# Reordering the second quad's scores and the sums in the first two attention stages of a fused attention and MLP kernel

## The chip, the cores and the metric

The kernel runs on one core of a Trainium2 chip. The metric is the device time of one execution in microseconds (us); lower is better. Engines: PE is TensorE (matrix products), ACT is ScalarE, DVE is VectorE, POOL is GpSimd, SP is SyncE, which here only issues the stores of the result.

## The reference

Attention with 32 global and 512 local tokens for 8 batches of 8 heads, and behind it a two-layer MLP with a sigmoid gelu. The attention output of a batch (544 rows of 8 x 64) is the MLP's input. Local tokens see the global keys and the local keys within 32 positions; global tokens see everything.

```python
k_all = concat([k_g, k_l], axis=2); v_all = concat([v_g, v_l], axis=2)
out_g = softmax(scale * q_g @ k_all.T) @ v_all
s_ll = where(abs(pos[:, None] - pos[None, :]) <= 32, scale * q_l @ k_l.T, -1e9)
s_l = concat([scale * q_l @ k_g.T, s_ll], axis=-1)
out_l = softmax(s_l) @ v_all
x = concat([out_g, out_l], axis=2).transpose(0, 2, 1, 3).reshape(B * S, H * D)
h = x @ w_in                                # 512 -> 2048
g = h * (1 / (1 + exp(-1.702 * h)))
out = g @ w_out                             # 2048 -> 512
```

## The kernel before

The four heads of half a batch are a "quad". A quad stands for its heads on the four groups of 32 partitions. In the code `a` is the first quad of the batch in work and `c` the second. The kernel's own order of calls is the order of each engine's queue: nothing is rescheduled, and an engine that waits holds up everything behind it in its queue. Waits are placed by the tile framework, from which tiles an instruction reads and writes.

The steps of a quad:

- `T`, `Tq`, `Tk`, `ext` (DVE, some copies on ACT): queries and keys as loaded (`rq`, `rk`) are transposed and laid out; the global ones come from `qgT` and `kgT`.
- `S(rnd)` (PE): scores of the local keys in two rounds, into four PSUM banks, one for each head. In batch 0 (class `Quad`) `B(rnd)` puts a bias there first, with products by an identity, and `S` adds to it (`added=True`). A score target is either a pair of two-bank tiles (`spair()`, tags s0 and s1; `bank(pair, j)` is bank j % 2 of tile j // 2), or, with `split=True`, four single banks.
- `X(rnd)` (ACT): exponentials out of PSUM into the tile `e`, which is `E[rnd]`: two instructions on a pair, four on single banks.
- `M(rnd, eng)` (DVE unless told otherwise): from batch 1 on (class `Wide`) the exponentials are multiplied by a mask of ones and zeros.
- `U(unit)` (PE): unit 0 multiplies the exponentials by ones, which gives the softmax sums; units 1 and 2 multiply them by the two halves of the values. Batch 0 has global keys apart: `K` (scores), `XK` (exponentials), `ekU(unit)` (their share of each unit, accumulated in the same bank).
- `R` (DVE): transpose `sT` out of the bank of unit 0, reciprocal `rT`, transpose `rs`.
- `XL(h)` (DVE): bank of unit 1 + h times `rs`, into the MLP's input `xL`.
- `eg`, `Gm`, `G`: the same for the 32 global queries.

PSUM has eight banks: four singles that rotate (`pbank`, tag p), and the pairs s0 and s1, one buffer each. A new tile in a buffer waits until the old one has been read.

The MLP of a batch follows as sixteen hidden tiles (`h_mm` into a bank, L611; `gelu` into `gT`, L616), each the sum of four products of 512 columns, and the second product (`o_mm`, L651; from batch 2 on a scheme with fewer products, L722). While the second product of batch i runs, the attention steps of batch i + 1 are called between its parts (`osteps`); `o_out` copies a finished tile of the output out of PSUM, and SP issues its stores.

Loads are issued by POOL. `behind(c.E[1][...])` (L624) is a one-element copy on POOL that reads the second quad's masked exponentials, so that the loads called after it (batches 2 and 3) are issued only when these are done. Their `rk` and `rq` go through `Tk`, `Tq` and `transpose_g`; the first quad's `ext` of batch 2 is on ACT between the gelus of batch 1.

Lines that the text names: L335 `B`, L352 and L556 `S`, L371 `K`, L380, L383 and L567 `X`, L407 `XK`, L419 `ekU`, L434 and L582 `U`, L452 and L593 `Gm`, L458 to L462 `R`, L467 `XL`, L572 `M`, L508 `Tk`, L772 the copy of an output tile on DVE, L81 and L82 the loads of `rq` and `rk`, L225 the copies that build the mask, L113 a copy on ACT.

Of the kernel before, what the change touches and what calls it, by code (L numbers as in the profile page):

```python
# [20 lines left out]
def kernel(  # L21
# [12 lines left out]
    nc = tc.nc  # L34
# [246 lines left out]
    def spair():  # L281
        return [psS.tile([128, 2, 512], F32, name="s4", tag="s%d" % i) for i in range(2)]

    def bank(pair, j):
        return pair[j // 2][:, j % 2, :]
# [358 lines left out]
    def o_mm(i, st, out=True):  # L644
        tci, f4 = divmod(st, 4)
        first = (i, tci) not in ops
        if first:
            ops[i, tci] = pbank("op")
        op = ops[i, tci]
        for fc in range(4 * f4, 4 * f4 + 4):  # L650
            nc.tensor.matmul(op, lhsT=gTs[i][:, fc, tci * 128 : tci * 128 + 128],  # L651
                             rhs=w_out_sb[:, fc, :], start=(first and fc == 4 * f4), stop=(fc == FC - 1))
        if f4 == 3 and out:
            o_out(i, tci, op)
# [102 lines left out]
    def tile_out(i, tci, ob, engs=4 * (nc.sync,), cols=slice(0, d_model)):  # L757
        for j, eng in enumerate(engs):
            if i < B:
                rows = out[i * S + Sg : (i + 1) * S, cols].rearrange("(r t) m -> t r m", t=16)[4 * tci + j]  # L760
            else:
                r = (4 * tci + j) * S
                rows = out[r : r + Sg, cols]
            eng.dma_start(out=rows, in_=ob[32 * j : 32 * j + 32])
# [3 lines left out]
    def o_out(i, tci, op, copy=on_act):  # L768
        if tci % 2 == 0:
            obs[i, tci // 2] = moe.tile([128, 4, HM], F32, name="ob", bufs=3)  # L770
        ob = obs[i, tci // 2][:, tci % 2 * 2 : tci % 2 * 2 + 2].rearrange("p h m -> p (h m)")
        copy(ob, op)  # L772
        tile_out(i, tci, ob)

    a, c = Quad(0), Quad(1)
# [35 lines left out]
    c.B(0)  # L811
    a.K()
    a.XK()
    c.S(0, added=True)
    c.X(0)
    a.eg()
    a.U(0)
    a.ekU(0)
    a.R()
    pt = spair()  # L820
    c.B(1, split=True, more=[bank(pt, 0)])
    c.S(1, split=True, added=True)
    c.X(1)
    a.ekU(1)
    a.U(1)
    a.XL(0)
    c.K()
# [6 lines left out]
    pt = spair()  # L834
# [22 lines left out]
    def osteps(i, *sts):  # L857
        for tci, f4 in sts:
            o_mm(i, 4 * tci + f4)

    nq = {1: (Wide(2), Wide(3)), 2: (Wide(4), Wide(5))}
    a, c = nq[1]
# [19 lines left out]
    c.S(0)  # L882
    c.X(0)
    osteps(0, (0, 3), (1, 3))
    c.M(0)
    o_mm(0, 11, False)
    o_out(0, 2, ops[0, 2], nc.vector.tensor_copy)
    c.S(1)
    c.X(1)
    for unit in range(3):  # L890
        a.U(unit)
    a.R()
    c.M(1)
    behind(c.E[1][0:1, 0, 32:34])
    load(2, (0,))
# [3 lines left out]
    load_v(2)  # L899
    osteps(0, (3, 2), (3, 3))  # L900
    pt = spair()
    a.XL(0)
    a.XL(1)
    a.Gm(bank(pt, 1)[:, 0:128])
    c.Gm(bank(pt, 1)[:, 128:256])
    c.U(0, bank(pt, 0))
    c.R()
    c.U(1, bank(pt, 2))
    c.U(2, bank(pt, 3))
    c.XL(0)  # L910
    c.XL(1)
    gTs[1] = moe.tile([128, FC, TB], BF16, name="gT")
# [9 lines left out]
    pt = spair()  # L922
# [3 lines left out]
    a, c = nq[2]  # L926
# [154 lines left out]
    for i in range(1, B):  # L1081
        if i > 1:
            for fc in range(FC):
# [3 lines left out]
                if i + 1 < B:  # L1087
                    c = nq[i + 1][1]
# [108 lines left out]
```

## Time and profile before

| | |
|---|---|
| median of 3 runs | 291.94 us (291.76 to 292.04) |
| profiled execution, its own time | 292.44 us |
| span of the profiled execution, first to last instruction | 290.4 us |
| PE busy | 277.3 us, 95% |
| DVE busy | 204.2 us, 70% |
| ACT busy | 184.2 us, 63% |
| POOL busy | 94.0 us, 32% |
| mean granted PE clock | 0.995 |

Times in the profile count from the first instruction of the span. The attention of batch 0 takes the first 18 us, its hidden layer lasts to about 33 us, its second product with the attention of batch 1 to about 52 us, and the hidden layer of batch 1 to about 67 us. A timeline row gives start, duration, engine, line, operation, output<-inputs, shapes and how many instructions were merged; the idle time of the engine before it is in brackets, with what ended it. Some records of matrix products are missing, so that a row can show one product too few.

### The profile page before, as it was taken

The page shows a single profiled execution, that of the slowest core. Times are in us where ns is not written, and L with a number is a line of the kernel's source. Part 1 is how long each engine was busy: PE and PEld are TensorE (multiplying, and loading weights), DVE is VectorE, ACT ScalarE, POOL GpSimd, SP SyncE. Part 2 cuts the span into 40 slices and gives each one's busy share as a digit, 9 for nine tenths or more (in the row PEclk, how much of TensorE's full clock was granted, in tenths as well). Part 3 has the DMA queues.
Part 4 walks back from the last instruction along what each step waited for, and adds up shares of the span by engine and source line. Part 5 has one row for each costly group of instructions (what it writes and reads, how often), then busy time and mean ns, then how long its engine had stood idle before and what let it go on. Part 6 is the DMA issues. An engine that isn't in the chain of part 4 may idle for free.

```text
span 290.4 us, 8836 instructions
## 1 busy us (share of the span) xinstructions
PE 277.3 (95%) x3704; PEld 178.5 (61%) x3727; DVE 204.2 (70%) x494; ACT 184.2 (63%) x296; POOL 94.0 (32%) x140
## 2 busy tenths in 40 slices
PE   6899999999999999999999999999999999999990
PEld 5544445544554488647874588548864787468880
DVE  7670456788689898679957995889865885454360
ACT  4747747388778684878658765878477834763330
POOL 8884550766946003910095006600210000000000
PEclk9999999999999999999999999999999999999998
DMA  7999993999999802991169503910121012200232
GB/s 200 160 205 211 203 140 58 156 224 134 157 187 157 146 3 68 94 194 30 34 75 175 106 5 75 144 21 2 48 72 30 2 29 67 54 2 0 75 85 61
DMA packets 59736, 28.23 MB, mean 97 GB/s; under 512 B 47665, under 2 KB 50225, under 8 KB 59697
## 3 DMA queue, kind: packets, MB, share of 16 engines
q0 software_dynamic: 51664, 17.57, 55.1%
q1 hardware_dynamic: 7552, 9.45, 11.9%
q8 instruction: 29, 0.48, 0.7%
q10 hardware_dynamic: 480, 0.66, 0.7%
q14 instruction: 11, 0.08, 0.1%
HBM read 36.31 MB, written 8.91 MB: 156 GB/s over the span
## 4 chain that ended last, share of the span: by engine, by line
PE 90%; DVE 2%; DMA 2%; POOL 1%; issue 1%; ACT 1%; DVEq 0%; POOLq 0%
PE hp L611 37%; PE px L722 13%; PE py L722 9%; PE op L651 9%; PE x L722 6%; PE s L556 6%; PE ov L582 5%; PE s L611 2%; DMA rk<-in_k_l_dram 2%; DVE xL L467 1%; ACT e L380 1%; PE og L593 1%; DVE rs L462 0%; DVE sT L458 0%; PE s L352 0%
## 5 line engine op out<-in xcount | busy, mean ns | idle before, releaser
L611 PE MATMUL hp<-xL,w_in_sb 128*128 128x512 bf16 x465 | 104.7, 379 | 1.2 <-DVE xL L467 0.4
L611 PEld LDWEIGHTS <-w_in_sb 128*128 128x128 bf16 x576 | 56.1, 98 | 60.4 <-issue 0.7
L616 ACT ACTIVATE gT<-hp 128x512 bf16<-128x512 f32 x120 | 69.8, 597 | 20.8 <-PE hp L611 19.3
L567 ACT ACTIVATE e<-s 128x1016 bf16<-128x1016 f32 (+1 forms) x56 | 53.3, 1003 | 22.9 <-PE s L556 22.9
L722 PEld LDWEIGHTS <-gs 128*128 128x128 bf16 x480 | 46.2, 98 | 6.5
L695 DVE TENSOR_TENSOR gs<-gT 128x512 bf16<-128x512 bf16 (+1 forms) x90 | 30.3, 364 | 17.4 <-ACT gT L616 17.2
L572 POOL TENSOR_TENSOR e<-e,mask 128x1760 bf16<-128x1760 bf16 x4 | 13.3, 3318 | 82.6 <-ACT e L567 82.6
L98 POOL DMA_DIRECT2D v<-in_v_l_dram x40 | 31.2, 784 | 15.9 <-DMA rk<-in_k_l_dram 5.3
L722 PE MATMUL py<-wsum,gs 128*128 128x256 bf16 x240 | 30.3, 273 | 0.0
L572 DVE TENSOR_TENSOR e<-e,mask 128x1712 bf16<-128x1712 bf16 (+1 forms) x24 | 25.0, 1043 | 6.9 <-ACT e L567 6.9
L651 PE MATMUL op<-w_out_sb,gT 128*128 128x512 bf16 x122 | 28.8, 380 | 0.5 <-issue 0.3
L508 DVE STREAM_TRANSPOSE kT<-rk 128x512 f32<-128x512 f32 x14 | 14.6, 1046 | 14.7 <-DMA rk<-in_k_l_dram 14.7
L651 PEld LDWEIGHTS <-gT 128*128 128x128 bf16 x128 | 11.8, 98 | 13.9
L722 PEld LDWEIGHTS <-gT 128*128 128x128 bf16 x192 | 18.0, 98 | 2.7
L722 PE MATMUL px<-w_out_sb,gT 128*128 128x256 bf16 x160 | 19.2, 273 | 0.0
L722 PE MATMUL px<-w_out_sb,gs 128*128 128x256 bf16 x160 | 19.1, 273 | 0.0
L467 DVE TENSOR_TENSOR xL<-ov,rs 128x512 bf16<-128x512 f32 x27 | 17.9, 686 | 0.8 <-PE ov L434 0.4
L692 DVE TENSOR_TENSOR gs<-gT 128x1024 bf16<-128x1024 bf16 (+1 forms) x30 | 17.4, 578 | 0.0
L556 PEld LDWEIGHTS <-kT 32*128 32x128 bf16 x672 | 12.6, 93 | 7.3 <-issue 5.9
L113 ACT ACTIVATE ob<-px 128x512 f32<-128x512 f32 x10 | 6.0, 597 | 15.2 <-DVE zz L744 15.2
L556 PE MATMUL s<-q,kT 32*128 32x160 bf16 (+1 forms) x448 | 15.0, 246 | 0.0
L100 POOL DMA_DIRECT2D v<-in_v_g_dram x24 | 14.0, 584 | 1.7 <-DMA rq<-in_q_l_dram 1.7
(149 smaller groups left out, 341.2 us busy)
## 6 DMA issues: line engine op xcount, KB each, us to landing
out_dram<-ob SPq DMA_DIRECT2D x128, 64.0 KB, 2.6
rq<-in_q_l_dram POOLq DMA_DIRECT2D x5, 512.0 KB, 8.3
rk<-in_k_l_dram POOLq DMA_DIRECT2D x5, 512.0 KB, 10.3
v<-in_v_l_dram POOLq DMA_DIRECT2D x24, 96.0 KB, 4.6
w_in_sb<-in_moe_w_in_dram POOLq DMA_DIRECT2D x8, 256.0 KB, 7.4
w_out_sb<-in_moe_w_out_dram POOLq DMA_DIRECT2D x4, 512.0 KB, 10.0
rq<-in_q_l_dram POOLq DMA_DIRECT2D x5, 256.0 KB, 8.4
rk<-in_k_l_dram POOLq DMA_DIRECT2D x5, 256.0 KB, 7.9
```

Source lines behind the costliest of these rows:

```text
L98: nc.gpsimd.dma_start(out=vt[0:n, hs, c, :D], in_=vs[FIRST[c] : FIRST[c] + n, hs])
L467: nc.vector.tensor_mul(self.x[:, 2 * self.u + h, :], self.st[1 + h], self.st["rs"])
L508: nc.vector.transpose(flat[:, 0:Sl].rearrange("p (r t) -> p t r", t=16), loaded[self.b][0][:, self.u].bitcast(F32))
L556: nc.tensor.matmul(bank(self.ps, j)[:, at : at + n], lhsT=self.k[p, KEYS[c] : KEYS[c] + 128, e], rhs=qs[p, :, :, e], start=(e == 0), stop= ...
L567: nc.scalar.activation(self.E[rnd][:, 2 * i : 2 * i + 2, :n], self.ps[i][:, :, :n], AF.Exp, scale=scale)
L572: eng.tensor_mul(e, e, mask[:, rnd : rnd + 1, :n].to_broadcast([128, 4, n]))
L611: nc.tensor.matmul(hp[:, : width(i)], lhsT=w_in_c[:, fc // 4, kc, fc % 4 // 2, :, fc % 2], rhs=(xL[i] if i < B else xG)[:, kc, :], start=( ...
L616: nc.scalar.activation(out_, in_, AF.Gelu_apprx_sigmoid)
L651: nc.tensor.matmul(op, lhsT=gTs[i][:, fc, tci * 128 : tci * 128 + 128], rhs=w_out_sb[:, fc, :], start=(first and fc == 4 * f4), stop=(fc = ...
L692: nc.vector.tensor_tensor(sums[i][2][:, g, :n], t[:, g, 0, :n], t[:, g, 1, :n], ALU.add)
L695: nc.vector.tensor_tensor(sums[i][k][:, g, : n // 2], x[:, g], y[:, g], op)
L722: nc.tensor.matmul(out_, lhsT=lv[:, g, tt * 128 : tt * 128 + 128], rhs=rv[:, g, :], start=(g == 0 and k in ((1, 3, 4, 6) if self.apart els ...
```

## The change

In batch 0 most bias products of `c`'s second score round are called ahead of `c.S(0)`, the rest and the second round itself directly after it. The first quad's sums follow behind that round. The first quad's three accumulators lie in a score pair; the four single banks go to the second quad's scores. `ekU(unit)` comes ahead of `U(unit)` in unit 0 as well.

In the second product of batch 0, where the attention of batch 1 is computed, `c.M(0)` runs on POOL. `a.U(0)` and `a.R()` are called ahead of `c.S(1)`, and `a.XL(0)` ahead of `c.M(1)`. The two `Gm` are called after the second quad's units.

```diff
@@ batch 0
     c.B(0)
     a.K()
     a.XK()
+    c.B(1, split=True, js=range(3))
     c.S(0, added=True)
     c.X(0)
-    a.eg()
-    a.U(0)
-    a.ekU(0)
-    a.R()
-    pt = spair()
-    c.B(1, split=True, more=[bank(pt, 0)])
+    c.B(1, split=True, js=(3,))
     c.S(1, split=True, added=True)
     c.X(1)
-    a.ekU(1)
+    a.eg()
+    pt = spair()
+    a.ekU(0, bank(pt, 0))
+    a.U(0)
+    a.R()
+    a.ekU(1, bank(pt, 1))
     a.U(1)
     a.XL(0)
     c.K()
     c.XK()
     a.ekU(2, bank(pt, 2))
     a.U(2)
     a.XL(1)
     a.Gm()
@@ batch 0's second product
     c.S(0)
     c.X(0)
     osteps(0, (0, 3), (1, 3))
-    c.M(0)
+    c.M(0, nc.gpsimd)
     o_mm(0, 11, False)
     o_out(0, 2, ops[0, 2], nc.vector.tensor_copy)
+    a.U(0)
+    a.R()
     c.S(1)
     c.X(1)
-    for unit in range(3):
-        a.U(unit)
-    a.R()
+    a.U(1)
+    a.U(2)
+    a.XL(0)
     c.M(1)
     behind(c.E[1][0:1, 0, 32:34])
     load(2, (0,))
...
     load_v(2)
     osteps(0, (3, 2), (3, 3))
     pt = spair()
-    a.XL(0)
     a.XL(1)
-    a.Gm(bank(pt, 1)[:, 0:128])
-    c.Gm(bank(pt, 1)[:, 128:256])
     c.U(0, bank(pt, 0))
     c.R()
     c.U(1, bank(pt, 2))
     c.U(2, bank(pt, 3))
+    a.Gm(bank(pt, 1)[:, 0:128])
+    c.Gm(bank(pt, 1)[:, 128:256])
     c.XL(0)
     c.XL(1)
```

## The prediction

> **What bounds the kernel now.** I read the page first: TensorE (PE) is busy 95% of the span, and section 4 gives it the chain.
>
> ```profile
> span 290.4 us, 8836 instructions
> ...
> ## 4 chain that ended last, share of the span: by engine, by line
> PE 90%; DVE 2%; DMA 2%; POOL 1%; issue 1%; ACT 1%; DVEq 0%; POOLq 0%
> ```
>
> So only what stops PE, or starts a long run of its products later, can move the end. Next, who PE waits for (columns: total us, times, longest); after the first kernel stage one wait is left, on VectorE (DVE):
>
> ```profile
> engine line waited for: us in total, times, longest us
> PE s L352 <- DVE q L313: 1.9, 1, 1.9
> ...
> PE s L352 <- DVE eg L393: 0.6, 1, 0.6
> PE hp L611 <- DVE xL L467: 0.4, 1, 0.4
> ```
>
> The 0.6 lies where the first edit is, the 0.4 where the second is. Third, the timeline of the first place (start, length, engine, line; in brackets the idle time before):
>
> ```profile
> 9.86 1.82 ACT L380 ACTIVATE e<-s 128x428 bf16<-128x428 f32 x4
> 11.76 0.66 PE L352 MATMUL s<-q,kT 32*128 32x200 bf16 x16 [0.55 <-DVE eg L393]
> 12.46 1.66 ACT L383 ACTIVATE e<-s 128x856 bf16<-128x856 f32 x2 [0.29 <-PE s L352]
> 13.11 0.81 PE L335 MATMUL s<-bias,ident 128*128 128x192 bf16 x8
> 13.22 0.72 DVE L458 STREAM_TRANSPOSE sT<-ov 128x512 f32<-128x512 f32 x1 [1.47 <-PE ov L419]
> 14.46 0.40 PE L419 MATMUL ov<-ek,rvg 32*32 32x512 bf16 x4
> 14.54 1.81 ACT L380 ACTIVATE e<-s 128x428 bf16<-128x428 f32 x4 [0.42 <-PE s L352]
> 16.89 0.40 PE L419 MATMUL ov<-ek,ones 32*32 32x512 bf16 x4 [0.16 <-ACT ek L407]
> ```
>
> ScalarE (ACT) idles 0.42 ahead of the second quad's second exponentials, waiting for its scores: that is what the first edit addresses. Fourth, the second place and what hangs on it:
>
> ```profile
> 47.67 0.68 DVE L772 COPY ob<-op 128x512 f32<-128x512 f32 x1
> 50.12 1.01 DVE L572 TENSOR_TENSOR e<-e,mask 128x1712 bf16<-128x1712 bf16 x1
> 51.20 0.17 POOL L624 COPY spot_p<-e 1x2 bf16<-1x2 bf16 x1 [8.04 <-DVE e L572]
> 51.97 0.55 POOL L82 DMA_DIRECT2D rk<-in_k_l_dram  x1
> 54.84 1.89 PE L611 MATMUL hp<-xL,w_in_sb 128*128 128x512 bf16 x8 [0.45 <-DVE xL L467]
> 59.06 1.06 DVE L508 STREAM_TRANSPOSE kT<-rk 128x512 f32<-128x512 f32 x1 [2.35 <-DMA rk<-in_k_l_dram]
> 61.52 0.31 ACT L113 ACTIVATE q<-qgT 128x128 bf16<-128x128 bf16 x1 [1.08 <-DVE qgT L243]
> 62.85 0.59 ACT L616 ACTIVATE gT<-hp 128x512 bf16<-128x512 f32 x1
> 63.49 0.38 PE L611 MATMUL hp<-xL,w_in_sb 128*128 128x512 bf16 x1
> ```
>
> Read it upwards. The last row is the first product of hidden tile 12 of batch 1; it takes the PSUM bank of tile 8, whose gelu (62.85) ends at 63.44. PE issues a product each 0.216 (16 of them take 3.62, less 0.38 for the last) and would have been there at 63.47, so this place is level, without slack. That gelu stands in ACT's queue behind L113, which waited for qgT, behind kT on DVE, which waited for the DMA of rk. That DMA was issued behind POOL's one-element copy L624, which waits for the second quad's second mask product (50.12 to 51.13). So **when c.M(1) ends** sets PE at 63.49, whatever PE gains at 54.84.
>
> **First edit, the scores of c in batch 0.** No instruction is added. Six of the eight bias products of c.B(1) now go ahead of c.S(0), two behind it; a's sums, their reciprocal R and c's second round change places, and a's three accumulators move from single banks into the score pairs.
>
> Start of c.S(0): the four single banks rotate; c.B(1)'s third product needs the bank that a.X(1)'s fourth exponential reads, to 9.86+1.82=11.68. With 0.05 from an end to PE's start (the bias product at 10.02 follows an exponential that ended at 9.97) it runs at 11.73; three more of 0.07 to 0.08 and 0.16 for the change to the score shape put c.S(0) at 12.11, not 11.76: +0.35. The 0.55 idle before it covers only the first two.
>
> X(0) moves to 12.81-14.47. X(1) no longer waits for its scores and follows at 14.36: -0.18. a.ekU(0) waits for the first half of X(0) (13.69) and runs at 13.74; a.U(0) follows 0.32 later and ends at 14.56. R's first transpose takes 14.61-15.33.
>
> Now the step that decides. a.ekU(1) writes bank 1 of the pair whose bank 0 that transpose reads, and stands after it in the program. The framework orders accesses by tile, and the pair is one tile: the product gets a wait for the transpose. In the kernel before these sums lie in tiles of their own. No row of before shows such a wait, so its bounds are 0 (ordered by bank, start at 14.50) and 0.88 (start at 15.38, from 15.33+0.05); I take the upper, since that is how tiles are declared here. Queued behind it on PE are a.U(1), c.K, a.ekU(2), a.U(2), a.Gm, c.U(0) and c.ekU(0). In the trace PE alone needs 16.66-14.46=2.20 from a.ekU(1) to c.ekU(0) (16.50, the last c.U(0) product, and 0.16). So c.ekU(0) comes at 17.58, against 16.89. ACT's exponential of c.K would end at 17.44: hidden. The first layer of batch 0 then starts **0.69 later**, at 19.30 (18.61 before: its row says 18.83, with 15 of 16 products recorded at 0.216). DVE hides under that: c.R at 18.03, c.XL(0) done at 20.58; the ninth product, which reads it, comes at 19.30+8x0.216=21.03. From there to 43 us the trace shows PE waiting for nothing, and no load of that stretch has its landing changed: 0.69 goes through.
>
> **Second edit, in times of before.** c.M(0) moves from DVE (1.08) to POOL. POOL's four such products take 3.32 each (page, L572 POOL): 46.7 to 50.0. Who needs it is c.U(0), at 51.0 at the earliest: hidden with 1.0 to spare, and L624 and the loads, queued behind it on POOL, wait longer for c.M(1).
>
> DVE: the copy L772 waits for its products (47.36) instead of c.M(0): 47.41-48.09. a.U(0) runs from 47.29 (24 products, 0.55). sT at 48.01, rs ends at 49.76 (R took 48.45 to 50.20, 1.75), a.XL(0), now ahead of c.M(1), 49.86-50.55. c.M(1) can start at 50.47. ACT says the same: c.S(1) now stands behind a.U(0), 0.48 later, and c.X(1) ends at 50.38. So c.M(1) ends at 51.48 instead of 51.13: **+0.35**, although DVE has 1.08 less to do. L624 and the eight loads behind it on POOL start 0.35 later. SP's stores keep their distance: the copy's 0.3 gain falls while SP still issues the tile before.
>
> PE: c.U(0) ends at 51.92, c.R's transpose takes 52.00-52.71, and the two Gm (40 products, 0.41), which write the other bank of that pair, wait for it by the same rule, to 52.76. The first layer of batch 1 starts at 53.24 instead of 52.49, and its ninth product comes at 54.97, without the 0.45 wait (c.XL(0) is done at 54.53): +0.13. The load path is later, +0.35, so it sets PE at hidden tile 12.
>
> **A rule weighed.** In the trace POOL's mask copies (14.43-16.76) ran over DVE's SBUF-to-SBUF transpose at 14.26; it took 0.71, as the one at 18.37 did without them. The Trainium skill (Advanced Engine Details and Errata, VectorE Performance Modes, Mode Summary) says that VectorE's second SBUF port is shared with GpSimd and that two-port VectorE instructions and GpSimd's block each other. By that rule the end would be as in the third rival; the rows here speak against it, for this transpose.
>
> **Sum.** 0.69 + 0.35 = +1.04 from hidden tile 12 of batch 1 to the end, where before PE waits for nothing. The profiled execution (292.44: span 290.4 and 2.04 around it) would be 293.5, span 291.4; it is 0.50 above the median of 291.94, so the median becomes **293.0**. If the DMA of rk does not land later with its issue, PE's 0.13 takes the place of 0.35: 292.8. If it lands up to 0.4 later still (stores run beside it), 293.4.
>
> **Rivals.**
> Waits by bank, not by tile (not slower, 15%): a.ekU(1) starts at 14.50, c.ekU(0) at 16.71. But a.XL(1), behind the later R, ends at 17.75, c.R follows, c.XL(0) is done at 20.21, and the ninth product runs at 20.26 instead of 20.34: -0.08. With +0.35 this is +0.27: 292.2. It decides if a.ekU(1) starts before 15.3. For it: PE's row L419 at 14.46 needed no such wait; against it: there the sums had a tile each.
> Loads free as well (faster, 6%): if also c.M(1)'s end did not matter, the wait at 54.84 would be won: -0.08 and some -0.3, 291.6. Against: the level rows at 63.4.
> The port (6%): if DVE's reciprocal transpose at 49.05 had to let POOL's product end first (50.0), c.M(1) came another 1.0 later: 294.0.
>
> **Chances.** Forecast 73% (292.7 to 293.4), rivals as above. Range 292.1 to 293.6: forecast and first rival. A measurement of this kernel tells about 0.2% (0.58 us) from no change: slower 0.77, same 0.17, faster 0.06.
>
> **What would show it.** Right: c.X(1) follows c.X(0) without idle time; PE idles about 0.8 before L419's second group, ended by DVE sT; L611 starts near 19.3; POOL's L572 near 47.4; L624 near 52.2; PE's wait for xL gone and one for ACT at hidden tile 12. Wrong: L419 close on L434, or PE going through tile 12 without a wait.

## The result, and the profile after

The change makes the kernel slower: 293.19 us (median of 13 runs) against 291.94; the ratio is 1.0042, with a 95% interval of 1.0024 to 1.0060, that is +1.2 us (0.7 to 1.8). The profiled execution took 293.37, with this span:

```profile
span 291.4 us, 8837 instructions
```

The waits of PE (us in total, times, longest):

```profile
PE s L352 <- DVE q L313: 1.2, 1, 1.2
...
PE s L419 <- DVE sT L458: 0.8, 1, 0.8
PE hp L611 <- ACT gT L616: 0.4, 1, 0.4
...
PE s L335 <- ACT e L380: 0.2, 1, 0.2
```

The 0.4 for `xL` is gone. In its place stand 0.8 for the transpose `sT`, in batch 0, and 0.4 for a gelu, at hidden tile 12 of batch 1. The timeline of batch 0 (start, length; idle time before in brackets):

```profile
9.58 1.82 ACT L380 ACTIVATE e<-s 128x428 bf16<-128x428 f32 x4
11.45 0.45 PE L335 MATMUL s<-bias,ident 128*128 128x192 bf16 x4 [0.18 <-ACT e L380]
11.83 0.66 PE L352 MATMUL s<-q,kT 32*128 32x200 bf16 x16
12.53 1.66 ACT L383 ACTIVATE e<-s 128x856 bf16<-128x856 f32 x2 [0.64 <-PE s L352]
14.07 1.82 ACT L380 ACTIVATE e<-s 128x428 bf16<-128x428 f32 x4
14.33 0.72 DVE L458 STREAM_TRANSPOSE sT<-s 128x512 f32<-128x512 f32 x1 [3.09 <-PE s L434]
15.10 0.40 PE L419 MATMUL s<-ek,rvg 32*32 32x512 bf16 x4 [0.82 <-DVE sT L458]
```

c.X(1) (14.07) follows c.X(0) without idle time, as the edit wants. But PE stands still from 14.28 to 15.10, until the transpose of the neighbouring bank has ended (15.05). And of the second stage:

```profile
47.20 3.33 POOL L572 TENSOR_TENSOR e<-e,mask 128x1760 bf16<-128x1760 bf16 x1 [3.55 <-ACT e L567]
50.85 1.04 DVE L572 TENSOR_TENSOR e<-e,mask 128x1712 bf16<-128x1712 bf16 x1
51.96 0.17 POOL L624 COPY spot_p<-e 1x2 bf16<-1x2 bf16 x1 [1.43 <-DVE e L572]
52.80 0.55 POOL L82 DMA_DIRECT2D rk<-in_k_l_dram  x1
60.17 1.05 DVE L508 STREAM_TRANSPOSE kT<-rk 128x512 f32<-128x512 f32 x1 [3.30 <-DMA rk<-in_k_l_dram]
62.62 0.31 ACT L113 ACTIVATE q<-qgT 128x128 bf16<-128x128 bf16 x1 [1.67 <-DVE qgT L243]
63.95 0.59 ACT L616 ACTIVATE gT<-hp 128x512 bf16<-128x512 f32 x1
64.59 1.89 PE L611 MATMUL hp<-xL,w_in_sb 128*128 128x512 bf16 x7 [0.44 <-ACT gT L616]
```

It is the chain of the prediction with every link later: mask product, POOL's copy, `rk`, `qgT`, gelu, and now PE visibly waits at its end, 1.10 later than before.

The start of the span differs by some tenths from run to run (a.X(1) began at 9.86 before and at 9.58 after), so the traces below are compared by intervals, from rows of each: **A** from the start of a.X(1) to the first gelu of batch 0; **C** from the end of c.X(0) in batch 1 to POOL's copy L624; **D** from the issue of the first `rk` behind it to its landing; **P** from the end of c.X(0) to the first gelu of batch 2. Between A and P lie 24.8 us in every trace, and behind P 203.4 to 203.6 us of the execution's time; so the start, A and P hold nearly all the differences between the profiled executions. The start (a.X(1) at 9.2 to 10.1) varies without regard to the edits.

| kernel | A | C | D | P | median us | ratio to before (95%) |
|---|---|---|---|---|---|---|
| before | 11.98 | 4.55 | 7.07 | 42.17 | 291.94 | |
| the change | 12.66 | 4.92 | 7.35 | 42.86 | 293.19 | 1.0042 (1.0024 to 1.0060) |
| e1, first edit alone | 12.67 | 4.54 | 7.05 | 42.14 | 293.09 | 1.0039 (1.0026 to 1.0052) |
| e2, second edit alone | 11.56 | 4.91 | 7.82 | 43.55 | 292.49 | 1.0015 (1.0001 to 1.0028) |
| e3, change, own tile | 11.89 | 4.91 | 6.44 | 42.27 | 292.29 | 1.0012 (1.0000 to 1.0025) |
| e4, only c.M(0) on POOL | 11.57 | 4.55 | 6.62 | 42.15 | 292.05 | 0.9998 (0.9989 to 1.0006) |
| e5, change, early loads | 12.66 | 3.55 | 5.69 | 42.26 | 293.31 | 1.0044 (1.0025 to 1.0063) |
| e6, before, early loads | 11.58 | 1.17 | 6.67 | 42.66 | 293.25 | 1.0049 (1.0025 to 1.0072) |
| e7, before, late loads | 11.57 | 5.75 | 5.80 | 42.37 | 293.21 | 1.0042 (1.0018 to 1.0066) |
| e8, first edit, own tile | 11.90 | 4.55 | 6.57 | 42.17 | 292.40 | 1.0008 (0.9997 to 1.0019) |
| e9, e8, bias behind | 12.13 | 4.54 | 7.19 | 42.32 | 291.94 | 0.9994 (0.9980 to 1.0008) |
| e10, e2, c.M(0) on DVE | 11.57 | 5.19 | 6.07 | 42.54 | 292.47 | 1.0012 (0.9999 to 1.0025) |

A, C, D and P are of one profiled execution each, which need not be a typical one; the medians are of 6 to 13 runs. e1 to e4, e5 to e7 and e8 to e10 each ran beside the kernel before, at 292.00, 291.99 and 292.09.

### The profile page after: what moved, and what is told of

Same layout as the page of the kernel before. It is cut to its first block, busy times and chain, and to the rows that moved or that the text cites. A ratio compares the mean times of both kernels' runs of the same rounds, so it can differ in the third digit from the quotient of the medians.

```text
span 291.4 us, 8837 instructions
## 1 busy us (share of the span) xinstructions
PE 278.2 (95%) x3704; PEld 178.7 (61%) x3727; DVE 203.4 (70%) x493; ACT 184.2 (63%) x296; POOL 97.4 (33%) x141
## 4 chain that ended last, share of the span: by engine, by line
PE 87%; DMA 4%; DVE 3%; ACT 2%; issue 1%; SPq 0%; POOL 0%; DVEq 0%
PE hp L611 35%; PE px L722 12%; PE py L722 9%; PE op L651 9%; PE x L722 6%; PE s L556 5%; PE ov L582 5%; DMA rk<-in_k_l_dram 3%; DMA early<-in_q_l_dram 2%; PE s L611 1%; PE og L593 1%; ACT e L380 1%; PE s L352 1%; ACT e L383 1%; ACT gT L616 0%
## 5 line engine op out<-in xcount | busy, mean ns | idle before, releaser
L616 ACT ACTIVATE gT<-hp 128x512 bf16<-128x512 f32 x120 | 69.8, 597 | 20.8 <-PE hp L611 19.3
L572 POOL TENSOR_TENSOR e<-e,mask 128x1760 bf16<-128x1760 bf16 x5 | 16.6, 3319 | 85.8 <-ACT e L567 85.8
L572 DVE TENSOR_TENSOR e<-e,mask 128x1712 bf16<-128x1712 bf16 (+1 forms) x23 | 24.0, 1043 | 5.4 <-ACT e L567 5.4
L467 DVE TENSOR_TENSOR xL<-ov,rs 128x512 bf16<-128x512 f32 x26 | 17.3, 686 | 0.5
```

The costliest lines, as they stand in the source:

```text
L467: nc.vector.tensor_mul(self.x[:, 2 * self.u + h, :], self.st[1 + h], self.st["rs"])
L572: eng.tensor_mul(e, e, mask[:, rnd : rnd + 1, :n].to_broadcast([128, 4, n]))
L616: nc.scalar.activation(out_, in_, AF.Gelu_apprx_sigmoid)
```

## The experiments

**e1: the first edit alone.** The first hunk of the diff is kept, the rest is as before.

> The first edit alone (batch 0); the second product of batch 0 as before. Theory (a.ekU(1) is made to wait for the transpose of the other bank of its pair): PE waits some 0.8 us ahead of L419, ended by DVE sT, the first layer starts 0.69 us later, and all of it goes through: about 292.6 by the before of 291.94. Rival (the cost of the whole change lies in the later mask product and the loads behind it, and the first edit costs nothing or gains 0.1): 291.8 to 292.0.

Measured +1.1 us (0.8 to 1.5), more than expected; its trace shows the 0.8 wait for `sT` and, as before, the 0.44 wait for `xL`. Most of the loss is in this edit. (The profiled execution, 292.43, is the quickest of the six: its a.X(1) starts at 9.24. A is 12.67 in it, as in the change.)

**e2: the second edit alone.** The first hunk is undone, the other two are kept.

> The second edit alone. Theory (c.M(1) ends 0.35 us later relative to the output tiles before it, the loads behind it start as much later, and hidden tile 12 of batch 1 waits for them): +0.35 to +0.6 us, 292.3 to 292.5, with PE's wait for xL gone and a wait for ACT at hidden tile 12. Rival (the loads have slack, PE's won wait counts): -0.3 us, 291.6. Rival (all of the loss is in the first edit): 291.9.

Measured +0.44 us (0.03 to 0.8): within what the theory gives, and hardly clear of no change. PE's wait for `xL` is gone and a wait for ACT at hidden tile 12 stands there, of 1.1 us in this execution, where `rk` took 7.82 to land. C is 0.36 longer than before.

**e3: the change with a.ekU(1) in the other pair.**

```diff
-    a.ekU(1, bank(pt, 1))
+    a.ekU(1, bank(pt, 2))
...
-    a.ekU(2, bank(pt, 2))
+    a.ekU(2, bank(pt, 1))
```

> The change with units 1 and 2 of the first quad exchanged between their banks, so that a.ekU(1) writes the other pair than the one that the transpose reads. No instruction more or less. Theory: PE's 0.8 us wait ahead of L419 goes, the first layer starts about 0.1 us earlier than before instead of 0.69 later, and the time falls by 0.7 to 0.8 us against the change: about +0.3 on before, 292.2 to 292.4. Rival (the order of the work, the later c.S(0) and the later sums, costs the time, not the wait): no more than 0.2 us below the change, 293.0.

Measured 292.29, 0.9 us below the change. The same place in the trace of e3:

```profile
14.49 0.40 PE L419 MATMUL s<-ek,rvg 32*32 32x512 bf16 x4
14.58 0.72 DVE L458 STREAM_TRANSPOSE sT<-s 128x512 f32<-128x512 f32 x1 [3.09 <-PE s L434]
15.35 0.40 PE L419 MATMUL s<-ek,rvg 32*32 32x512 bf16 x4
```

a.ekU(1) (14.49) no longer waits and starts even before the transpose. A falls by 0.77, from 12.66 to 11.89, by a choice of banks alone: the wait was made by the tile in which the accumulator lies. A small part of it moved to a.ekU(2), which now writes the other bank of the transposed tile: it starts at 15.35, 0.05 after the transpose has ended (15.30), and 0.86 after a.ekU(1) instead of 0.77 as in the change (15.87 - 15.10). In e8 and e9 it starts 0.05 after the transpose as well. Here `rk` also landed early (6.44), and PE has no wait at hidden tile 12: P is 42.27, 0.1 above before. So the time is as expected, but it is made up otherwise: A lies 0.3 above the 11.57 of the kernels without the first edit, where 0.1 less was expected, and P only 0.1 above before.

**e4: only c.M(0) on POOL.**

```diff
-    c.M(0)
+    c.M(0, nc.gpsimd)
     o_mm(0, 11, False)
```

> The kernel before with only c.M(0) moved to GpSimd. Theory: nothing, as a.R waits for a.U(0) behind c.S(1) in any case and c.M(1) starts at the same time: within 0.1 us of before, 291.94; DVE's transposes under the POOL product take the same 0.71 us. Rival (shared port): the transpose rs or the POOL product gets longer and c.M(1) with all behind it comes up to 0.6 us later: 292.5.

Measured 292.05, a ratio of 0.9998. DVE and POOL in the trace of e4:

```profile
46.26 3.33 POOL L572 TENSOR_TENSOR e<-e,mask 128x1760 bf16<-128x1760 bf16 x1 [3.92 <-ACT e L567]
...
47.91 0.72 DVE L458 STREAM_TRANSPOSE sT<-ov 128x512 f32<-128x512 f32 x1 [0.36 <-PE ov L582]
...
48.95 0.71 DVE L462 STREAM_TRANSPOSE rs<-rT 128x512 f32<-128x512 f32 x1
49.58 1.01 DVE L572 TENSOR_TENSOR e<-e,mask 128x1712 bf16<-128x1712 bf16 x1
```

The first transpose ran wholly under POOL's product and the second all but its last 0.07, at their usual length (in the change both lie wholly under it, with 0.71 each), and the product took its usual 3.3: no contention, and no gain either, since DVE now idles 0.36 for a.U(0). The move by itself is free.

**e5, e6, e7: the loads' gate.** In e5 (on the change) and e6 (on the kernel before) POOL's copy reads the first round of exponentials; in e7 it reads xL, one step after c.M(1).

```diff
-    behind(c.E[1][0:1, 0, 32:34])
+    behind(c.E[0][0:1, 0, 32:34])        # e5, e6
+    a.XL(0)                               # e7, moved up from behind the output tiles
+    a.XL(1)
+    behind(xL[1][0:1, 1, 0:2])
```

> The change with POOL's copy ahead of the loads reading c's first masked exponentials instead of the second, so that the loads of batch 2 are issued about 1.4 us earlier (at 50.6 in its trace instead of 52.2). Theory: rk lands earlier by about as much, hidden tile 12 of batch 1 no longer waits for ACT, and PE's own path counts: 0.69 from the first edit and 0.13 from the second, so 0.3 to 0.6 us below the change, about 292.7. Rival (the loads do not set it): the time of the change, 293.2.

> The kernel before with the same earlier loads (behind c.M(0), 3.4 us earlier). Theory: PE reached hidden tile 12 of batch 1 just as its bank came free, so nothing is won: 291.9, with PE's wait of 0.45 for xL still there. Rival (before also waits on the loads by more than the trace shows): 0.3 us faster or more.

> The kernel before with the same loads issued later: POOL's copy reads the first quad's second half of xL, which DVE finishes 1.2 us after c.M(1). The order on DVE is unchanged. Theory: all of it reaches the end through rk, qgT on ACT and hidden tile 12: +1.1 to +1.3 us, 293.1. Rival (the loads have slack): 291.9 to 292.2.

In e5 the trace does what the theory says: PE's wait at hidden tile 12 is gone and P is 42.26, 0.60 less than in the change and 0.1 above before, so without the load path the second edit is worth +0.1 on PE. (The first `rk` is issued 1.1 us earlier after c.X(0), 4.67 against 5.75, and landed 1.66 quicker.) The time missed its forecast, 293.31 and not 292.7. That forecast took the first edit at 0.69; with the 1.1 of e1 and the 0.1 it would be 293.2. Against the change the time did not fall, so how far the wait at hidden tile 12 counts in the median of the change is not shown.

e6 missed too: 293.25 where no change was expected. DMA in 48.5 to 52.6, first of before and then of e6 (packets, MB, share of 16 engines):

```profile
DMA packets 315, 0.46 MB, mean 112 GB/s; under 512 B 98, under 2 KB 98, under 8 KB 314
...
q8 instruction: 1, 0.02, 1.9%
```

```profile
DMA packets 405, 0.69 MB, mean 168 GB/s; under 512 B 76, under 2 KB 76, under 8 KB 404
...
q8 instruction: 1, 0.02, 3.6%
```

One 16 KB packet of instructions took 3.6% of 16 x 4.1 us = 2.4 us instead of 1.25, beside loads that now fill the DMA engines. And PE stops twice with nothing that the profile shows to wait for:

```profile
52.52 0.35 PE L582 MATMUL s<-e,v 128*32 128x72 bf16 x9 [0.29 <-issue]
83.06 0.55 PE L582 MATMUL ov<-e,v 128*32 128x128 bf16 x24 [0.34 <-issue]
```

The first stop costs nothing: it takes the place of the wait for `xL`, which is gone, and the products of hidden tile 4 start 9.91 after c.X(0), as before. The 0.5 by which P is longer arises at the second stop: ACT's exponentials shortly before it come as long after c.X(0) as before (35.45 and 35.49), the next ones 0.5 later (38.88 and 38.38). That the slow packet made these stops is not shown, and the rows speak against it: it began before 49.3 and so had ended by 51.7, half a us before PE stopped; the second stop follows a packet of the usual 1.3; and packets of 1.8 (the change) and 1.9 (e5) have no such stop behind them. The profiled execution is the quickest of e6's twelve, 0.7 above the median of before, and P accounts for most of that; what makes the median 1.3 higher is open.

e7 was 1.2 us slower (0.5 to 1.9), as expected. Its trace does not show the path: PE has no wait at hidden tile 12, and P is 0.2 longer. That execution was one of its quickest, 291.99 of runs from 291.89 to 294.91, and there `rk` landed 5.80 after its issue instead of 7.07.

**e8: the first edit alone, with the banks of e3.**

> The first edit alone, with units 1 and 2 of the first quad exchanged between their banks (no wait of a.ekU(1) for the transpose); the second product as before. The traces so far give, from the start of a.X(1) to the first gelu of batch 0: 11.57 us in three kernels whose first edit is left out, 12.66 with it, 11.89 with it and the banks exchanged. Theory (the wait is 0.77 of the 1.1 us, the bias products ahead of c.S(0) the rest): 11.89 again and +0.3 us on before, 292.3. Rival (the wait is all of it): 292.0.

A is 11.90, as the theory has it, and the time +0.2 us (-0.1 to +0.6): too little to tell 0.3 from 0, so the split rests on A. The 0.3 that is left in A holds the 0.09 by which a.ekU(2) comes later (see e3).

**e9: e8 with all bias products behind c.S(0).**

```diff
-    c.B(1, split=True, js=range(3))
     c.S(0, added=True)
     c.X(0)
-    c.B(1, split=True, js=(3,))
+    c.B(1, split=True)
```

> As e8_scores_own_tile, with all eight bias products of c's second round behind c.S(0) instead of six ahead of it. Theory (c.S(0) was held by the third bias product's bank, so now scores and exponentials come as early as the keys allow): c.X(0) starts 2.2 us after a.X(1) instead of 2.95, from a.X(1) to the first gelu 11.3 to 11.6 us, time 291.8 to 292.0. Rival (the later sums of the first quad cost the 0.3): 11.9 and 292.3, as e8.

Measured 291.94, 0.5 us below e8 and level with before (ratio 0.9994). Its trace can't confirm the reason: in that execution c's queries and keys came late and PE waited 0.85 for them ahead of c.S(0), so A is 12.13 and c.X(0) starts 2.89 after a.X(1), not 2.2. The time leans to the theory, though the runs of the two overlap (e8 from 291.92 to 292.81, e9 from 291.43 to 292.83); the rows speak neither for it nor against it. It is the form of the first edit with the lowest median here, and no measurable gain.

**e10: the second edit with c.M(0) left on DVE.**

> The second edit alone with c.M(0) left on DVE. Theory (DVE's queue sets the end of c.M(1)): c.M(1) ends 0.25 us later than with c.M(0) on GpSimd, 0.6 later than before, and time 0.2 to 0.3 us above the second edit alone, about 292.6 to 292.8. Rival (ACT's exponentials behind the later c.S(1) set it): as the second edit alone.

C is 5.19, 0.28 longer than in e2, so with c.M(0) on DVE its queue does set the end of c.M(1). The medians are the same (292.47 and 292.49), where 0.2 to 0.3 more was expected. In this execution `rk` landed after 6.07 and nothing waited for it; P is 0.4 above before all the same, as PE waited 0.45 for c.M(1) itself, ahead of the last products of c.U(0) (0.18 in e2).

## Why the prediction was right

**Way and size.** Forecast was 293.0 with a span of 291.4; measured were 293.19 and 291.4. The mechanism that was given the most weight, a wait by tile and not by bank, is shown by the trace (0.82, ended by `sT`) and by e3, which takes it away with a bank number (A down by 0.77). The size is in part luck, as the next paragraphs show.

**First edit, a term that was too small.** The sum had 0.69 for it, and between the two profiled executions A does grow by 0.68. But e1 costs 1.1 us, and A of the kernels without this edit is 11.56 to 11.58 in five traces of six; only the one that the sum was made from has 11.98. There c's keys landed late. First the row of before, then two of e4:

```profile
10.66 1.04 DVE L309 STREAM_TRANSPOSE kT<-rk 128x512 f32<-128x512 f32 x1 [1.22 <-DMA rk<-in_k_l_dram]
```

```profile
9.94 1.06 DVE L309 STREAM_TRANSPOSE kT<-rk 128x512 f32<-128x512 f32 x1 [0.47 <-DMA rk<-in_k_l_dram]
11.05 0.66 PE L352 MATMUL s<-q,kT 32*128 32x200 bf16 x16
```

The transpose of the keys starts 0.80 after a.X(1) in before and 0.21 after it in e4. In before it ends at 11.70, and the 0.55 of PE's idle time ahead of c.S(0) ends with it, though the profile names `eg` (in e4 c.S(0) starts before `eg` does, at 11.05 and 11.16). The sum took that wait for a fixture of the kernel, and let the later c.S(0) cost only 0.35 on top of it. Where the keys come in time, c.S(0) starts 1.32 after a.X(1) (e4). In the change it starts 2.25 after it, as worked out, held not by the keys but by a bias product that waits for a.X(1)'s bank (11.45). So the edit costs 12.66 - 11.57 = 1.09: 0.77 that the choice of banks takes away and 0.32 for the rest. For the same reason the rival without the wait was given -0.08, and e3 and e8 show +0.3 in A.

**Second edit.** c.M(1) ends 0.37 later after c.X(0) (C), forecast 0.35, though DVE lost a product of 1.08. In the change c.X(1) ended at 50.77 and a.XL(0) at 50.93, so ACT and DVE bound it nearly alike, as worked out; e10 shows DVE's part. PE's own path is +0.1 where the loads come in time (e3, e5), forecast 0.13. That the loads set the end is shown for the profiled execution of the change by the 0.44 at hidden tile 12, and by e5, where it goes with an earlier gate. How much of it counts hangs on D, which the sum took as fixed: over these traces it runs from 5.7 to 7.8 us. At 6.44 (e3) nothing waits, at 7.35 (the change) 0.44, at 7.82 (e2) 1.1. So +0.35 is no constant. In the medians the second edit costs 0.44 alone (e2), but only 0.1 on top of the first edit (the change against e1) and nothing on top of e8 (e3); by the intervals of the table these differences are uncertain by half a us or so, and the size of this term in the time is not shown.

**The sum.** The single edits add to 1.1 + 0.4 = 1.5, with intervals that hold the measured 1.2. The forecast 1.04 had its first term 0.4 too small. The last step made the same mistake once more: it took off 0.50 because the profiled execution before lay that far above the median, but 0.41 of this is the late keys in A (11.98 against 11.57), which the change does not feel. With 1.09 in place of 0.69 the sum gives 293.4, with the old term 293.0, and 293.19 lies between them. That the span of 291.4 was met is luck as well: between the two profiled executions A grew by 0.68, as forecast, P by 0.69 where 0.35 was forecast, since `rk` landed 0.28 slower, and a start 0.28 earlier took most of that back.

**The rivals.** By bank: refuted by the wait and by e3. Loads without weight: refuted for the profiled executions of the change and of e2 by PE's wait for ACT, and e7's time speaks against it; for the medians it is not settled. The port: in e4 the transposes under POOL's product kept 0.71 and 0.72. The rule of the Trainium skill weighed there (Advanced Engine Details and Errata, VectorE Performance Modes, Mode Summary) did not show for these instructions, of which no run shows whether they use both ports; a DVE product of two SBUF inputs under a POOL product was not tried (in e4 c.M(1) starts at 49.58, and POOL ends at 49.59).

**The expected marks.** c.X(1) behind c.X(0) without idle time, the 0.8 ahead of L419, POOL's L572 at 47.2, L624 at 51.96, the wait for `xL` gone and one for ACT at hidden tile 12: all there. The first layer starts at 19.01, forecast 19.3, in an execution in which a.X(1) starts 0.28 earlier.

## What to carry to other kernels

Look at the tile, not at the bank: an accumulator moved into a two-bank tile inherits the waits of whatever reads the other half, and the order of calls that was harmless with one tile each becomes a stop of PE. When work is moved off an engine, follow the result that ends last, not the engine's busy time: here DVE lost 1.08 us, the mask product that gates the next loads still came 0.37 later, and the 0.4 wait for `xL` won on PE came back as a wait of 0.44 at the end of the load path. And before a wait in one trace is used as cover for an edit, ask whether it is a fixture: a DMA that landed late once makes an edit look cheap.

## What the runs showed that was not expected

The landing of a load of 256 KB took from 5.7 to 7.8 us after its issue in kernels that differ little there, so a path that is level in one execution is late in the next. Earlier loads were no gain: on the kernel before they cost 1.3 us, on the change they won nothing measurable. With the DMA engines filled (e6, 168 GB/s instead of 112), a 16 KB packet of instructions took 2.4 us instead of 1.25. PE stood still twice in that trace, for 0.29 and 0.34 us, with no wait that the profile shows; the cause is open. And GpSimd's product of 3.33 us left the transposes of VectorE beside it at their length.
